# Four later modulation vectors: one row in four column groups, spread through memory

## The chip, the cores and the metric

The kernel runs on one core of a Trainium2 chip. The core has a matrix engine (TensorE, PE in the profile; its weight loads are listed apart as PEld), a vector engine (VectorE, DVE), an activation engine (ScalarE, ACT), a general engine (GpSimd, POOL) and an engine that here does nothing but issue transfers (SyncE, SP). Each of them takes its instructions in the order in which the program wrote them and waits where a semaphore says so. The metric is the time of one execution on the device, in microseconds (us); lower is better.

## The reference, cut to what matters

```python
mod = (_silu(c) @ w_mod).reshape(c.shape[0], 6, 1, -1)      # c: 1x512, w_mod: 512x3072
sa, ca, ga, sb, cb, gb = (mod[:, 0], mod[:, 1], mod[:, 2], mod[:, 3], mod[:, 4], mod[:, 5])
h = _layernorm(x, axis=-1) * (1 + ca) + sa                  # x: 1x2048x512
x = x + ga * _A_ref(h, A_wqkv, A_wo)                        # softmax attention, 32 heads of 16
h = _layernorm(x, axis=-1) * (1 + cb) + sb
x = x + gb * _B_ref(h, B_w1, B_b1, B_w2)                    # dense 512 -> 1792, mish, dense -> 512
return x
```

The six modulation vectors of 512 numbers each are numbered 0 to 5 in the kernel: `sa`, `ca` are 0 and 1, the gate `ga` is 2, the second shift `sb` is 3, the second scale `cb` is 4, the gate `gb` is 5. All of it is in float32; the large products take each operand as a high and a low part and add three products.

## The kernel before, in words

The kernel has a prologue (norm, transposes, the first K and Q slices), one long loop, and a tail. The loop goes in steps. A step of the main part makes, for one group of four heads, four score products of 512 columns whose results the activation engine turns into exponentials (lines 587 and 590), and beside them four more for a later group, of which the vector engine takes row maxima (lines 538 and 540). Two at a time stand on the two halves of the array's rows, and the results go through a ring of six PSUM banks. The step ends with `pv` (line 605): four float32 products of the exponentials with V, each in its own group of 32 array columns. In the slots beside the score products lies a unit of other work, cut in pieces: here the remaining Q, K and V slices (line 138, or line 131 outside the slots).

What is to be done beside the steps is hung on half-steps: `at(h, f)` runs `f` when the writing of the program comes to half-step `h`. All engines' programs are written in this one order, and there is no scheduler behind it. The transfers are all issued by SP, in the order in which they were written; with each the program also waits until the transfer that SP issued eight places earlier has landed, since eight completion slots are used in turn.

The modulation vectors 0 and 1 are made in the prologue. The other four are made in the loop, one after the other, in the order `(2, 5, 3, 4)`. For each, two pieces of `w_mod` are loaded (`mod_load`, line 699; `wm`), GpSimd multiplies them by `silu(c)` and adds the four row blocks (lines 703 to 705), which leaves a 128x512 tile whose columns are still to be summed over the 128 partitions. Six half-steps after the second piece `mod_unit` is written as a special at the end of a step, just ahead of `pv`. It sums over partitions on the matrix engine, into one bank of the ring:

- for a gate (2 and 5) the weights are a 128x128 tile of ones and the tile streams through, twice 256 columns. Every partition then holds the whole vector, and the activation engine copies the bank into the tile `gate` (line 722);
- for shift and scale (3 and 4) the tile itself is the weights, four blocks of 128x128, and one column of ones streams through each. The 512 sums then lie down the partitions in four columns, and the vector engine copies them into `modc` (lines 724 and 726).

Gate 0 is multiplied into the output weights and gate 1 into the second dense layer's weights (`prep_unit`, line 737), which are prepared in the loop later; columns 2 and 3 of `modc` are used when the second norm is applied (line 922). After the last of the four vectors `start_preps` begins the chain of these preparations.

Of the kernel before, what the change touches and what calls it, by code (L numbers as in the profile page):

```python
# [8 lines left out]
F32 = mybir.dt.float32  # L9
F32R = mybir.dt.float32r  # L10
AF = mybir.ActivationFunctionType
# [7 lines left out]
def adaln_block(ctx: ExitStack, tc: tile.TileContext, x, wqkv, wo, w1, b1, w2, c, w_mod, out):  # L19
    nc = tc.nc  # L20
    P = 128
    S, D = x.shape[1], x.shape[2]
# [3 lines left out]
    DK = D // P  # L26
# [27 lines left out]
    dram = ctx.enter_context(tc.tile_pool(name="dram", bufs=1, space=DRAM))  # L54
# [18 lines left out]
    ones = cst.tile([P, 1], F32, name="ones")  # L73
# [9 lines left out]
    modc = cst.tile([P, 4, DK], F32, name="modc")  # L83
    sil = cst.tile([P, DK], F32, name="sil")
    b1c = cst.tile([P, FT], F32, name="b1c")
    gates = [cst.tile([P, D], F32, name=f"gate{i}") for i in range(2)]

    def dap(t, off, ap):
        return bass.AP(tensor=t.tensor, offset=t.offset + off, ap=ap)
# [36 lines left out]
    def mm(acc, l, r, start, stop):  # L126
        pe_queue.append((acc, l, r, start, stop))
# [27 lines left out]
    def ring(w=1):  # L155
        if w == 2 and ring_at[0] % 2:
            ring_at[0] += 1
        if kept and ring_at[0] % NRING == NRING - 1:
            ring_at[0] += 1
        b = ring_at[0] % NRING  # L160
        ring_at[0] += w
        return ring_t[:, b, :] if w == 1 else ring_t[:, b:b + 2, :]
# [41 lines left out]
    def at(h, f):  # L204

        hooks.setdefault(h, []).append(f)
# [22 lines left out]
    def slice_load(kind, i, pool=None, lp=None):  # L229
        w = P if kind < 2 else 2 * P  # L230
        raw = (pool or qp).tile([P, DK, w], F32, tag="raw" if pool is pw else "wr", name="wr", bufs=2 if lp else 1)
        o = kind * D + i * w
        nc.sync.dma_start(raw, wqkv[:, o:o + w].rearrange("(k p) m -> p k m", p=P))
        slices[kind, i] = raw
# [93 lines left out]
    with ExitStack() as es:  # L328
# [121 lines left out]
        for i in range(2):  # L450
            row = lp.tile([P, D], F32, tag="hf", name="row", bufs=6)
# [159 lines left out]
    st, mst = {}, {}  # L611
# [96 lines left out]

    def mod_unit(v):

        gate = v in (2, 5)
        acc, rows = ring(), [mst.pop(("wm", 2 * v + o))[:, 0] for o in range(2)]
        for o, row in enumerate(rows):
            if gate:
                mm(acc[:, o * 2 * P:(o + 1) * 2 * P], ones.to_broadcast([P, P]), row, True, True)
            else:
                for m in range(2):
                    mm(acc[:, 2 * o + m:2 * o + m + 1], row[:, m * P:(m + 1) * P], ones, True, True)

        def fin(h):  # L720
            if gate:
                nc.scalar.copy(gates[(v - 2) // 3], acc)
            elif v == 4:
                nc.vector.tensor_scalar_add(modc[:, v - 1, :], acc[:, :DK], 1.0)
            else:
                nc.vector.tensor_copy(modc[:, v - 1, :], acc[:, :DK])
        return fin

    def prep_unit(h, third, scr, src, gate):
# [683 lines left out]
        return fin  # L1413

    at(-2 * PRO, lambda: slice_load(*plan[2][1:3]))
    order = (2, 5, 3, 4)

    def first_mods(h, j=0):
        for o in range(2):
# [2 lines left out]
    def queue_mod(j):  # L1422
        def make():
            put = mod_unit(order[j])

            def fin(h):
                put(h)
                if j + 1 < len(order):
                    first_mods(h, j + 1)
                else:  # L1430
                    start_preps(h + 2)
            return fin

        queue_special(lambda: mst.get(("row at", 2 * order[j] + 1), 4 * T) + 6, make)
# [110 lines left out]
```

## Time and profile before

| what | value |
|---|---|
| time, median of 3 runs | 1693.89 us (1693.4 to 1694.09) |
| the profiled execution's own time | 1694.02 us |
| its span, first to last instruction | 1692.1 us |
| granted TensorE clock, mean | 0.999 |
| PE / DVE / ACT / POOL busy | 1671.4 / 1442.0 / 1354.5 / 821.1 us |
| transfers | 238.44 MB, mean 141 GB/s |

In rows of the timeline the first column is the start in us from the span's start, the second the length in us, then engine, line, operation, written tile, read tiles, array tile where the engine is PE (64*128 is half of the array's rows, 128*32 a group of 32 columns), shapes and count; in brackets stands how long the engine was idle before, and what ended it. A float32 product appears as two records of PE, so the four products of `pv` are eight. Rows of consecutive records of the same line are merged.

### The profile page before, as it was taken

To read this page: it belongs to the slowest core of one execution; us is meant where nothing else is said; L and a number is where in the kernel's file an instruction comes from. 1 tells how busy PE (TensorE), PEld (TensorE's weight loads), DVE (VectorE), ACT (ScalarE), POOL (GpSimd) and SP (SyncE) were. 2 spreads that over 40 slices of the span, in tenths; PEclk is the share of its full clock that TensorE was granted. 3 is DMA by queue.
4 is the path that set the end of the run, shared out by engine and by line. 5 is a ranking of instruction groups with operands and counts; after the bars stand their busy time and mean duration, and the time that the engine had idled before them with its cause. 6 is when DMAs were issued, how large, how long until landed. Compare 5 with 4: busy or idle time off the path is not lost.

```text
span 1692.1 us, 33739 instructions
## 1 busy us (share of the span) xinstructions
PE 1671.4 (99%) x12410; PEld 925.8 (55%) x12410; DVE 1442.0 (85%) x2371; ACT 1354.5 (80%) x2610; POOL 821.1 (49%) x843
## 2 busy tenths in 40 slices
PE   7999999999999999999999999999999999999999
PEld 5755665555444555555555455555555455555587
DVE  8888888888889888888889888888889888884377
ACT  6257777777778988888888998888888998888674
POOL 7556224665413564555323564555323565555443
PEclk9999999999999999999999999999999999999999
DMA  7877545777755343434355434424354533533261
GB/s 250 260 239 201 132 136 179 229 224 216 216 172 142 106 101 84 127 80 131 85 145 148 118 74 97 137 73 132 82 146 126 131 93 77 143 107 128 77 230 63
DMA packets 114029, 238.44 MB, mean 141 GB/s; under 512 B 23824, under 2 KB 49424, under 8 KB 107912
## 3 DMA queue, kind: packets, MB, share of 16 engines
q1 hardware_dynamic: 113864, 236.28, 49.5%
q8 instruction: 98, 1.61, 0.4%
q14 instruction: 67, 0.55, 0.1%
HBM read 179.95 MB, written 51.44 MB: 137 GB/s over the span
## 4 chain that ended last, share of the span: by engine, by line
PE 92%; DVE 3%; ACT 3%; DMA 1%; issue 1%; POOL 1%; SPq 0%; ACTq 0%; DVEq 0%; POOLq 0%
PE bk L605 29%; PE ring L587 22%; PE ring L538 20%; PE bk L138 10%; PE bk L131 3%; PE ring L131 2%; PE ring L1214 2%; DVE mx L540 2%; ACT pr L590 1%; PE ring L552 1%; DMA xt<-in_A_x 0%; PE ring L917 0%; PE ring L567 0%; PE ring L138 0%; DMA ka<-kscr 0%
## 5 line engine op out<-in xcount | busy, mean ns | idle before, releaser
L540 DVE TENSOR_REDUCE mx<-ring 128x1 f32<-128x512 f32 x1968 | 1222.9, 683 | 151.3 <-PE ring L538 137.9
L590 ACT ACTIVATE pr<-ring 128x512 f32<-128x512 f32 x2048 | 1078.3, 603 | 209.3 <-PE bk L138 116.4
L538 PE MATMUL ring<-ka,qa 64*128 64x512 f32 x1968 | 818.6, 429 | 1.3 <-ACT pr L590 1.1
L587 PE MATMUL ring<-qa,ka 64*128 64x512 f32 x2048 | 759.4, 402 | 2.2 <-ACT pr L590 2.0
L605 PE MATMUL bk<-pr,vg 128*32 128x512 f32 x4096 | 545.1, 605 | 0.0
L538 PEld LDWEIGHTS ring<-ka,qa 64*128 64x128 f32 x1968 | 350.8, 184 | 326.2 <-DVE mx L540 251.3
L587 PEld LDWEIGHTS ring<-qa,ka 64*128 64x128 f32 x2048 | 374.0, 184 | 193.1 <-DVE mx L540 112.2
L138 PE MATMUL bk<-h,w 64*128 64x512 f32 (+1 forms) x1080 | 278.1, 391 | 0.0
L138 PE MATMUL bk<-w,a_h 64*128 64x512 f32 x632 | 211.0, 413 | 0.0
L138 PEld LDWEIGHTS bk<-h,w 64*128 64x128 f32 x1080 | 178.8, 185 | 8.4 <-ACT pr L590 1.5
L605 PEld LDWEIGHTS bk<-pr,vg 128*32 128x32 f32 x4096 | 80.8, 108 | 136.1 <-issue 126.6
L138 PE MATMUL bk<-w,a_l 64*128 64x512 f32 x316 | 124.3, 393 | 0.0
L138 PEld LDWEIGHTS bk<-w,a_h 64*128 64x128 f32 x632 | 106.9, 185 | 3.9 <-ACT hb L795 0.8
L973 POOL TENSOR_TENSOR y<-yd,y 128x512 f32<-128x512 f32 x44 | 56.9, 1292 | 89.1 <-ACT yd L972 84.2
L807 POOL TENSOR_SCALAR qq<-ee 128x512 f32<-128x512 f32 x25 | 15.5, 619 | 169.3 <-ACT ee L801 169.3
L823 POOL TENSOR_TENSOR qq<-qq,rr 128x512 f32<-128x512 f32 x42 | 54.2, 1289 | 86.0 <-ACT rr L817 86.0
L809 POOL TENSOR_TENSOR hb<-hb,ee 128x512 f32<-128x512 f32 x42 | 54.1, 1289 | 79.6 <-DVE ee L805 77.7
L138 PE MATMUL bk<-w,o_hl 64*128 64x512 f32 x288 | 79.1, 405 | 0.0
L100 POOL TENSOR_TENSOR a_l<-hb,a_h 128x512 fp32r<-128x512 f32 x53 | 73.2, 1381 | 4.4
L138 PEld LDWEIGHTS bk<-w,a_l 64*128 64x128 f32 x316 | 58.4, 185 | 3.2
L97 POOL TENSOR_SCALAR qh<-qf 128x512 fp32r<-128x512 f32 x27 | 16.7, 620 | 88.9 <-ACT qf L261 75.2
L138 PE MATMUL bk<-h_h,wl 64*128 64x512 f32 x168 | 57.2, 420 | 0.2 <-ACT pr L590 0.2
(222 smaller groups left out, 1917.0 us busy)
## 6 DMA issues: line engine op xcount, KB each, us to landing
ka<-kscr SPq DMA_DIRECT2D x124, 384.0 KB
w<-w2scr SPq DMA_DIRECT2D x56, 512.0 KB
w<-w1scr SPq DMA_DIRECT2D x46, 512.0 KB
vg<-vscr SPq DMA_DIRECT2D x32, 552.0 KB
qa<-qscr SPq DMA_DIRECT2D x124, 100.0 KB
kscr<-qh SPq DMA_DIRECT2D x16, 512.0 KB
qscr<-qh SPq DMA_DIRECT2D x32, 256.0 KB
w2scr<-hl SPq DMA_DIRECT2D x14, 512.0 KB
```

The source lines that it names most:

```text
L100: (nc.gpsimd if eng == "p" else nc.vector).tensor_sub(lo, src, hi.bitcast(F32))
L131: nc.tensor.matmul(acc, l, r, start=start, stop=stop)
L138: i = nc.tensor.matmul(acc, l[64 * g:64 * g + 64], r[64 * g:64 * g + 64], start=start and not then, stop=bool(stop and then))
L538: nc.tensor.matmul(pm, qt[64 * s:64 * s + 64, qs * P:(qs + 1) * P], kt[64 * s:64 * s + 64, kb * TB:(kb + 1) * TB], start=True, stop=True)
L540: nc.vector.tensor_reduce(out=mxs[n][:, s, 4 * j + qs, kb:kb + 1], in_=pm, op=ALU.max, axis=AX.X)
L587: nc.tensor.matmul(p_, kt[64 * s:64 * s + 64, kc * P:(kc + 1) * P], qt[64 * s:64 * s + 64, :], start=True, stop=True)
L590: e = nc.scalar.activation(pr, p_, AF.Exp, scale=SCALE)
L605: nc.tensor.matmul(accs[n][32 * h:32 * h + 32, :], vgs[n][:, o:o + 32], pts.pop((t, h)), start=(kc == 0), stop=(kc == 15))
L809: (nc.vector if tail else nc.gpsimd).tensor_mul(hb, hb, ee)
L823: nc.gpsimd.tensor_mul(qq, qq, rr)
L973: nc.gpsimd.tensor_add(y[i], yd, y[i])
L1214: nc.tensor.matmul(po[i // 2][:, i % 2, :], l[:, s], w[:, r, :], start=(f == 0 and j == 0), stop=(f == FT - 1 and j == 2))
```

## The change

All four vectors now take the same path. The weights are a 128x32 tile of ones, and the four blocks of 128 columns of the summed tile stream through the four groups of 32 array columns, one block each. The bank then holds, in partitions 0, 32, 64 and 96, the four quarters of the vector (repeated in the 31 partitions behind each). The activation engine copies 128x128 of it into the first 128 columns of a gate tile (for vector 4 with one added). Two half-steps later a transfer takes the four partitions to a new scratch in memory, `mscr`, and ten half-steps after that a second transfer brings them back: for a gate as a row repeated on all 128 partitions, for shift and scale number by number into a column of `modc`. The order of the four vectors becomes `(3, 4, 2, 5)`, so that the gate tiles are free to hold the rows of shift and scale first.

```diff
     gates = [cst.tile([P, D], F32, name=f"gate{i}") for i in range(2)]
+    mscr = dram.tile([4, DK, P], F32, name="mscr")
...
     def mod_unit(v):
-        gate = v in (2, 5)
-        acc, rows = ring(), [mst.pop(("wm", 2 * v + o))[:, 0] for o in range(2)]
-        for o, row in enumerate(rows):
-            if gate:
-                mm(acc[:, o * 2 * P:(o + 1) * 2 * P], ones.to_broadcast([P, P]), row, True, True)
+        acc, ws = ring(), [mst.pop(("wm", 2 * v + o)) for o in range(2)]
+        rows, modt = [w[:, 0] for w in ws], gates[v // 4][:, :P]
+        for c in range(DK):
+            mm(acc[32 * c:32 * c + 32, :P], ones.to_broadcast([P, 32]), rows[c // 2][:, c % 2 * P:(c % 2 + 1) * P], True, True)
+
+        def fin(h):
+            if v == 4:
+                nc.scalar.activation(modt, acc[:, :P], AF.Identity, bias=ones)
             else:
-                for m in range(2):
-                    mm(acc[:, 2 * o + m:2 * o + m + 1], row[:, m * P:(m + 1) * P], ones, True, True)
-
-        def fin(h):
-            if gate:
-                nc.scalar.copy(gates[(v - 2) // 3], acc)
-            elif v == 4:
-                nc.vector.tensor_scalar_add(modc[:, v - 1, :], acc[:, :DK], 1.0)
-            else:
-                nc.vector.tensor_copy(modc[:, v - 1, :], acc[:, :DK])
+                nc.scalar.copy(modt, acc[:, :P])
+            dst = mscr[v - 2]
+
+            def spread():
+                if v in (2, 5):
+                    nc.sync.dma_start(gates[(v - 2) // 3], dap(dst, 0, [[0, P], [1, D]]))
+                else:
+                    nc.sync.dma_start(modc[:, v - 1, :], dst.rearrange("k p -> p k"))
+
+            at(h + 2, lambda: nc.sync.dma_start(dst, modt[::32, :]))
+            at(h + 12, spread)
         return fin
...
-    order = (2, 5, 3, 4)
+    order = (3, 4, 2, 5)
```

On the matrix engine the four blocks stay where they were, ahead of a `pv`. The third of them before the change, with the tile `wm` as weights and the ones streaming (rows name the written tile, then weights and streamed tile, then partitions by columns of the result; `ka`, `qa` are the K and Q tiles of the score products, `bk<-pr,vg` is `pv`):

```order
L587 MATMUL ring<-qa_108,ka_629 128x512
L587 MATMUL ring<-qa_109,ka_630 128x512
L538 MATMUL ring<-ka_104,qa_106 128x512
L131 MATMUL ring<-ones,wm 128x1 x4
L605 MATMUL bk<-pr,vg 32x512 x4
L587 MATMUL ring<-qa_109,ka_630 128x512
```

The same place after the change, where all line numbers are one higher:

```order
L588 MATMUL ring<-qa_109,ka_630 128x512
L588 MATMUL ring<-qa_110,ka_631 128x512
L539 MATMUL ring<-ka_105,qa_107 128x512
L132 MATMUL ring<-wm,ones 32x128 x4
L606 MATMUL bk<-pr,vg 32x512 x4
L588 MATMUL ring<-qa_110,ka_631 128x512
```

Nothing moved there; the four products are now of the same form as those of `pv`, 32 partitions each, and only 128 columns long.

On SP eight transfers come in. Before, between the second and the third vector's load, the last of four small transfers into a Q tile (`qa<-mt`), a load of weights (`wr`), and the loads of a pair of Q and K tiles for a later group of heads:

```order
L576 DMA qa_109<-mt 2x4x128
L233 DMA wr<-in_A_wqkv 128x4x128
L312 DMA qa_106<-qscr 50x512 x2
L321 DMA ka_104<-kscr 48x2048 x2
L699 DMA wm<-in_w_mod 128x4x256 x2
```

After:

```order
L577 DMA qa_110<-mt 2x4x128
L728 DMA modc<-mscr 128x4x1
L234 DMA wr<-in_A_wqkv 128x4x128
L313 DMA qa_107<-qscr 50x512 x2
L322 DMA ka_105<-kscr 48x2048 x2
```

The way back of the first vector, from memory into `modc`, now stands ahead of the loads of the pair (whose tiles are numbered one higher); its way out stands eight transfers earlier, ahead of a load of V. The other three vectors' transfers come in likewise in the next 70 us, and all others keep their order.

## Prediction

> **What bounds the kernel now.** I read the page first: the span, the busy shares, the chain that ended last.
>
> ```profile
> span 1692.1 us, 33739 instructions
> PE 1671.4 (99%) x12410; PEld 925.8 (55%) x12410; DVE 1442.0 (85%) x2371; ACT 1354.5 (80%) x2610; POOL 821.1 (49%) x843
> PE 92%; DVE 3%; ACT 3%; DMA 1%; issue 1%; POOL 1%; SPq 0%; ACTq 0%; DVEq 0%; POOLq 0%
> ```
>
> PE is busy in 99% of the span and holds 92% of the chain. A busy PE can still be waiting inside a stage, so I went to the stage that the change touches. The four vectors are summed between 124 and 199 us, and there the matrix engine's timeline tells the cost:
>
> ```profile
> 121.44 0.40 PE L538 MATMUL ring<-ka,qa 64*128 64x512 f32 x1
> 121.77 1.07 PE L605 MATMUL bk<-pr,vg 128*32 128x512 f32 x8
> ...
> 124.73 1.10 PE L131 MATMUL ring<-wm,ones 128*128 128x256 f32 x4
> 125.77 1.06 PE L605 MATMUL bk<-pr,vg 128*32 128x512 f32 x8
> ...
> 128.60 1.06 PE L605 MATMUL bk<-pr,vg 128*32 128x512 f32 x8
> ...
> 140.08 1.07 PE L605 MATMUL bk<-pr,vg 128*32 128x512 f32 x8
> 141.08 0.28 PE L567 MATMUL ring<-ident,mm 128*32 128x128 f32 x1
> 141.29 0.50 PE L538 MATMUL ring<-ka,qa 64*128 64x512 f32 x1
> ...
> 146.04 1.06 PE L605 MATMUL bk<-pr,vg 128*32 128x512 f32 x8
> ...
> 148.54 0.47 PE L538 MATMUL ring<-ka,qa 64*128 64x512 f32 x1
> 149.01 1.10 PE L131 MATMUL ring<-wm,ones 128*128 128x256 f32 x4
> 150.04 1.06 PE L605 MATMUL bk<-pr,vg 128*32 128x512 f32 x8
> ...
> 152.88 1.07 PE L605 MATMUL bk<-pr,vg 128*32 128x512 f32 x8
> ```
>
> The start of line 605 is the clock tick of a step. Four plain steps run from 128.60 to 140.08, so a plain step is 2.87 us. The steps that hold a gate's sum run from 121.77 to 125.77 and from 146.04 to 150.04: 4.00 each, 1.13 more than plain. The same two ticks for shift and scale:
>
> ```profile
> 170.13 1.06 PE L605 MATMUL bk<-pr,vg 128*32 128x512 f32 x8
> ...
> 173.09 1.02 PE L131 MATMUL ring<-ones,wm 128*128 128x1 f32 x8
> 174.04 1.06 PE L605 MATMUL bk<-pr,vg 128*32 128x512 f32 x8
> ...
> 194.36 1.07 PE L605 MATMUL bk<-pr,vg 128*32 128x512 f32 x8
> ...
> 197.32 1.02 PE L131 MATMUL ring<-ones,wm 128*128 128x1 f32 x8
> 198.27 1.07 PE L605 MATMUL bk<-pr,vg 128*32 128x512 f32 x8
> ```
>
> Both take 3.91, 1.04 more than plain. So all of a block's length lies on the path, and nothing else hides it: 1.13 + 1.13 + 1.04 + 1.04 = 4.34 us for the four. The steps just behind run a little faster than plain (125.77 to 128.60 is 2.83, 150.04 to 152.88 is 2.84), because the other engines have caught up; that gives back 0.03 to 0.04 a block, so the blocks cost 4.2 net. This is the most that the change can win on the matrix engine, and 0.25% of the time.
>
> **The matrix engine's part.** Removed are 4 records of 256 columns in each gate block and 8 records of one column, each with a full 128x128 weight load, in the others. Added are, in every block, 8 records of 128 columns in four column groups of 32. Their price is not in the trace, but the same form is, four times longer, in line 605. Its eight records seen in stretches (busy time, with the number of records under way in brackets, for PE and for the weight loads):
>
> ```profile
> 125.74:125.90 0.16, 0.13 (x4) 0.14 (x8) 1.00 0.00 0
> 125.90:126.22 0.32, 0.32 (x4) 0.02 (x4) 1.00 0.00 0
> 126.22:126.42 0.20, 0.20 (x8) 0.00 (x0) 1.00 0.00 0
> ```
>
> The four groups run at once: four records are under way from 125.77, the next four join at about 126.24, 0.47 later, and the eight weight loads are over in 0.16. The granted clock is 1.00. Line 605 as a whole holds the path for 1.00 (140.08 to 141.08). With 128 columns in place of 512 a wave's pitch is 0.47 / 4 = 0.12, two waves 0.24; what 605 has beyond two pitches (1.00 - 0.94 = 0.06) I keep whole. That gives 0.30 a block. Bounds: from below 0.21, what one lone record of 128 columns behind 32-wide weights holds (line 567, 141.08 to 141.29). From above the groups do not overlap and the eight records go at the pace of the eight one-column records of the old shift block (173.09 to 174.04, 0.12 each), which is 0.95 and wins almost nothing. I take 0.30, since line 605 is the nearest row: same array tile, same type, the same stream into four groups of one bank.
>
> The block also stands next to `pv`, which now has its form. The old block began 0.47 behind the last score product (148.54 to 149.01), `pv` alone begins 0.33 behind it (121.44 to 121.77). By block lengths only (from line 131's start to line 605's: 1.04, 1.04, 0.95, 0.95, together 3.98) the gain would be 3.98 - 1.2 = 2.8; by the steps, which also count those 0.14, it is 4.2 - 1.2 = 3.0. The Trainium skill (TensorEngine Tiling (Array Packing), Key Properties) says that a change of the tiling mode drains the array, while another tile of the same mode does not; the old order changes mode twice from score products to `pv`, the new one once. By that rule the 0.14 go too, and the trace's 0.47 against 0.33 agrees. I take 3.0.
>
> **The activation engine's part.** Two copies of 128x512 go, four of 128x128 come, and two small vector-engine copies go.
>
> ```profile
> 149.32 0.59 ACT L261 COPY qf<-bk 128x512 f32<-128x512 f32 x1
> 149.79 0.63 ACT L590 ACTIVATE pr<-ring 128x512 f32<-128x512 f32 x1
> 150.28 0.62 ACT L722 COPY gate<-ring 128x512 f32<-128x512 f32 x1
> 151.56 2.06 ACT L590 ACTIVATE pr<-ring 128x512 f32<-128x512 f32 x4 [0.67 <-PE ring L538]
> ```
>
> ```profile
> L290 ACT COPY vq<-bk x28: 367/370/395, 53.7 to 244.9; 128x256 f32<-128x256 f32 x28
> ```
>
> 512 columns cost 0.62 and 256 cost 0.37, so 128 cost about 0.25: 4 x 0.25 = 1.0 against 1.24. Cost at nothing: behind the gate copy ACT idles 0.67 until the next step's scores come. With the block 0.8 shorter these come at 150.8 instead of 151.56, while the copy ends at 150.28 + 0.25 = 150.53; 0.2 to spare. For the one copy with a bias I allow 0.46 (line 922, below, has scale and bias on the same shape); it ends at 150.74, still in time. If that cover is gone ACT is next to be late, by 0.2 at most a block, 0.8 in all. A gain beyond the block's length has no place here, since ACT waits for PE.
>
> **The eight transfers.** SP issues them, and behind each stands what SP has queued. Who would notice are the K and Q tiles that the score products wait for.
>
> ```profile
> 149.49 0.77 SPq L321 DMA_DIRECT2D ka<-kscr  x2
> ...
> 155.50 2.62 SPq L271 DMA_DIRECT2D qscr<-qh  x2
> ```
>
> ```profile
> L331 SPq DMA_DIRECT2D cc<-in_c x1: 449/449/449, 0.7 to 0.7; - x1
> L360 ACT ACTIVATE sil_e<-cc x1: 205/205/205, 2.9 to 2.9; 128x4 f32<-128x4 f32 x1
> ```
>
> ```profile
> 149.00:164.00 15.00, 15.00 (x142) 9.48 (x143) 11.91 (x20) 12.20 (x25) 8.62 (x8) 1.00 0.97 214
> ```
>
> ```profile
> 182.00:196.00 14.00, 14.00 (x138) 8.70 (x138) 12.48 (x24) 10.47 (x22) 3.50 (x3) 1.00 0.09 25
> ```
>
> The columns before the last two are busy engines and the clock; then come the DMA share and GB/s. `cc` is of the same form as the way back into `modc` (512 pieces of four bytes): issued at 0.7, in use at 2.9, so at most 2.2 us to land. It stands before the busy stretch of 149 to 164. The write of four half-kilobyte rows has 10 half-steps, 5 x 2.87 = 14 us, to land before it is read back. A gate's spread is 256 KB, at the 214 GB/s of the stretch 1.2 us; the first falls into 182 to 196, where transfers fill 9%. An issue costs SP about 0.45 (`cc`'s row). The new readers have time:
>
> ```profile
> L737 POOL TENSOR_TENSOR hl<-hl,gate x18: 1267/1278/1290, 293.7 to 451.1; 128x512 f32<-128x512 f32 x18
> L922 ACT ACTIVATE hf<-ring,modc x48: 448/462/487, 518.1 to 1297.3; 128x128 f32<-128x128 f32 x48
> ```
>
> Gates are first read at 293.7 and `modc` at 518.1, the last spread is issued six steps behind the last block, near 198 + 6 x 2.87 = 215. Cost: 0, between 0 and the rival below. The new order of the vectors costs nothing for the same reason. As eight slots are used in turn and eight transfers are added, all later transfers keep their slots.
>
> **Sum.** 4 x 0.30 - 4.2 = -3.0 us. The profiled execution took 1694.02 (1.9 around its span of 1692.1), the median is 1693.89; I subtract from the median: 1690.9.
>
> **Rivals.**
>
> *The block nearly vanishes.* The weight loads hide behind the stream and only two pitches remain, 0.22 to 0.24. Then the four steps save 4.34 - 0.9 = 3.4 to 3.5 and the time is 1690.4. For it: eight loads take 0.16 in all in line 605 and lie beside the stream. Against it: one record of line 567 alone holds 0.21. It decides from 0.24 a block downwards. A fifth of a per cent, 3.4 us, is about what a measurement of this kernel can tell from no change, so this is the case on the far side of that line.
>
> *The groups do not overlap, or ACT's copies hold the ring.* Then blocks are 0.95 or steps stay near 3.9, the gain is 0.1 to 1 and the time 1693.3. Against it: line 605's x4 rows. It is also the case that the change does not do what it says.
>
> *Slower: a pair of K and Q tiles comes late.* The K tile issued from 149.49 has landed by 155.50 + 2.62 = 158.1 (line 271 waits for its completion slots), and the first product on it is due at 162.5: the tick at 146.04, a long step, four plain ones and a `pv` (146.04 + 4.00 + 4 x 2.87 + 1.00). That leaves 4.4; with PE 1.5 earlier, 2.9. If small pieces clogged the queue in a stretch already 97% full, the steps would stand. To end slower by 0.2% the pair must be late by 2.9 + 3.0 + 3.4 = 9.3 us; at that point the time is 1697.3. For it: the full stretch. Against it: `cc`'s 2.2. The Trainium skill (DMA: Bandwidth & Descriptors, Specifications) says that pieces under 512 bytes are read, modified and written; that would make the pieces dearer, and no run here shows how much.
>
> **How the numbers follow.** The forecast, 2.2 to 3.4 saved, 0.55; nearly vanishing, 0.25; no overlap or ACT in the way, 0.12; slower, 0.08. Faster by over 0.2% is the second case, 0.25; within 0.2% are the first and third, 0.67; slower 0.08. The range reaches down to 1689.9 (the whole 4.2 gone would be 1689.7) and up to 1693.2, where the case without overlap begins; what lies outside is most of that and the slower one.
>
> **What would show it.** Right: blocks of eight records `wm,ones` of form 128*32 and 128x128, about 0.3 from their start to line 606's; ticks of 3.15 to 3.2 in these four steps; ACT's copies near 0.25 with idle time behind them; no new wait of line 539 or 588 on `ka` or `qa`; all steps after 205 us as before, 3 us earlier. Wrong: blocks near 0.95; a gap on PE around 160 or 210 us released by a transfer; or steps elsewhere that lengthen by as much.

## The result: 2.5 us less, and what the profile shows after

The median went from 1693.6 us (22 runs) to 1691.1 us (22 runs, 1690.0 to 1695.6): a ratio of 0.9987, 95% interval 0.9981 to 0.9993. That is 0.13% faster (0.07 to 0.19%): a gain, and inside the 0.2% that was called no change. The profiled execution took 1691.02 us. The page of the kernel after:

```profile
span 1689.2 us, 33772 instructions
PE 1667.3 (99%) x12418; PEld 921.5 (55%) x12418; DVE 1441.5 (85%) x2369; ACT 1355.1 (80%) x2612; POOL 821.1 (49%) x843
PE 91%; DVE 3%; ACT 3%; DMA 2%; POOL 1%; issue 1%; SPq 0%; ACTq 0%; DVEq 0%; POOLq 0%
```

PE's share of the chain of waits fell from 92 to 91%, that of transfers rose from 1 to 2%: a first hint that something was given back. The timeline of PE around the second and the third block (all line numbers are one higher, so `pv` is line 606 and the block line 132):

```profile
143.80 1.06 PE L606 MATMUL bk<-pr,vg 128*32 128x512 f32 x8
...
146.30 0.47 PE L539 MATMUL ring<-ka,qa 64*128 64x512 f32 x1
146.76 0.43 PE L132 MATMUL ring<-wm,ones 128*32 128x128 f32 x8
146.98 1.07 PE L606 MATMUL bk<-pr,vg 128*32 128x512 f32 x8
...
149.83 1.07 PE L606 MATMUL bk<-pr,vg 128*32 128x512 f32 x8
...
167.07 1.06 PE L606 MATMUL bk<-pr,vg 128*32 128x512 f32 x8
...
169.60 0.43 PE L539 MATMUL ring<-ka,qa 64*128 64x512 f32 x1
170.03 0.42 PE L132 MATMUL ring<-wm,ones 128*32 128x128 f32 x8
170.25 1.07 PE L606 MATMUL bk<-pr,vg 128*32 128x512 f32 x8
```

From tick to tick these steps take 3.18 (143.80 to 146.98, 167.07 to 170.25), where they took 4.00 and 3.91. From the block's start to `pv`'s there are 0.22 in both: two waves of 0.11, where a wave is four records, one in each column group, that run at once. The lead, from the last score product to the block, is 0.46 (146.30 to 146.76), where it was 0.47.

The activation engine beside the same two blocks:

```profile
147.55 0.63 ACT L591 ACTIVATE pr<-ring 128x512 f32<-128x512 f32 x1
148.04 0.39 ACT L719 ACTIVATE gate<-ring,ones 128x128 f32<-128x128 f32 x1
148.52 2.07 ACT L591 ACTIVATE pr<-ring 128x512 f32<-128x512 f32 x4
...
171.13 0.28 ACT L721 COPY gate<-ring 128x128 f32<-128x128 f32 x1
171.78 2.06 ACT L591 ACTIVATE pr<-ring 128x512 f32<-128x512 f32 x4 [0.37 <-PE ring L539]
```

A plain copy takes 0.28 and ACT then idles 0.37 until the next scores. The copy with a bias takes 0.39; it ends 0.09 before the next exponential starts, so it is just in time. On SP, with four of the eight transfers:

```profile
160.17 0.52 SPq L730 DMA_DIRECT2D mscr<-gate  x1
167.84 0.50 SPq L728 DMA_DIRECT2D modc<-mscr  x1
...
189.38 0.39 SPq L726 DMA_DIRECT2D gate<-mscr  x1
200.02 0.55 SPq L730 DMA_DIRECT2D mscr<-gate  x1
```

Their issues cost SP 0.39 to 0.55 each, and no engine waited for one of the eight. One wait of PE for a transfer is in the trace, though, far behind the blocks, and the first trace of before has none there:

```profile
380.46 0.47 PE L588 MATMUL ring<-qa,ka 64*128 64x512 f32 x1 [1.24 <-DMA qa<-mt]
```

A product of scores waits 1.24 us for the small transfers (`qa<-mt`) that put four maxima into a Q tile. What this wait has to do with the change is the second question of the experiments; the first is what the block and the transfers cost each by itself.

### The profile page after: what moved, and what is told of

The parts are those of the page before. It is cut to its first block, busy times and chain, and to the rows that moved or that the text cites. A ratio compares the mean times of both kernels' runs of the same rounds, so it can differ in the third digit from the quotient of the medians.

```text
span 1689.2 us, 33772 instructions
## 1 busy us (share of the span) xinstructions
PE 1667.3 (99%) x12418; PEld 921.5 (55%) x12418; DVE 1441.5 (85%) x2369; ACT 1355.1 (80%) x2612; POOL 821.1 (49%) x843
## 4 chain that ended last, share of the span: by engine, by line
PE 91%; DVE 3%; ACT 3%; DMA 2%; POOL 1%; issue 1%; SPq 0%; ACTq 0%; DVEq 0%; POOLq 0%
PE bk L606 29%; PE ring L588 22%; PE ring L539 20%; PE bk L139 11%; PE bk L132 3%; PE ring L1219 2%; PE ring L132 2%; DVE mx L541 2%; ACT pr L591 1%; PE ring L553 0%; DMA qa<-mt 0%; DMA xt<-in_A_x 0%; PE ring L922 0%; DMA kscr<-qh 0%; PE ring L568 0%
```

## The experiments

In all of them the ticks (the starts of `pv`) are compared one by one with those of the first trace of before. That splits a kernel's distance from it into parts: the first tick, which lies before the first product, copy or transfer that the change alters; the gain between the first tick and the 35th (near 210 us), which holds the four blocks; what is lost between the ticks near 377 and 432 us, where the waits of PE for transfers lie; and all else up to the last tick, where a gain is positive and a loss negative. The whole table first, in us:

| kernel | first tick at | gain over the four blocks | lost near 380 to 430 | all else | median, and ratio to before |
|---|---|---|---|---|---|
| before, first trace | 110.36 | 0 | 0 | 0 | |
| before_again | 111.74 | 0.04 | 0.02 | 0.00 | 1695.37 (1 run) |
| before_third | 109.08 | 0.04 | 1.18 | -0.10 | 1693.97 (1 run) |
| before_fourth | 109.53 | -0.02 | 2.39 | -0.40 | 1695.98 (1 run) |
| after | 108.95 | 3.13 | 1.19 | -0.16 | 1691.11, 0.9987 (0.9981 to 0.9993) |
| again | 110.61 | 3.17 | 1.36 | -0.14 | 1691.71, 0.9983 (0.9973 to 0.9992) |
| again_third | 110.45 | 3.14 | 0.34 | -0.30 | 1691.79 (1 run) |
| no_transfers | 109.69 | 3.16 | 1.09 | 0.16 | 1690.61, 0.9973 (0.9963 to 0.9983) |
| transfers_only | 109.45 | 0.02 | 0.60 | -0.28 | 1694.55, 0.9994 (0.9985 to 1.0004) |
| behind_pv | 109.94 | 3.41 | 0.63 | -0.23 | 1691.52, 0.9982 (0.9972 to 0.9992) |
| double_block | 109.47 | 2.30 | 0.53 | -0.29 | 1691.84 (1 run) |
| two_groups | 113.34 | 1.70 | 1.78 | -0.12 | 1697.41 (1 run) |
| long_block | 111.28 | -0.35 | 0.88 | -0.24 | 1696.61 (1 run) |

The ratios are to the kernel before run beside each: 1693.6 for the first result, 1694.84 (28 runs) for again, no_transfers, transfers_only and behind_pv. Of the others one run of before stood beside: 1695.59 with double_block, two_groups, before_again and before_third, and 1694.05 with long_block, before_fourth and again_third, which ran on another chip. The first tick alone varies by 2.7 us between traces of the same kernel (109.08 to 111.74 for before). The gain over the blocks repeats to 0.04 us. So single times say little here, and the column of the blocks says much. The after of the first result has 1.4 us from its prologue that the change didn't give.

**The change once more (again).** The kernel after, unaltered, timed beside the three that follow.

> The changed kernel unaltered, once more. In its first trace the four blocks save 3.1 us against the trace of before, the prologue ended 1.4 us earlier, and 1.3 us were given back at 379 us, where a score product waited 1.2 for a transfer into a Q tile (`qa<-mt`). Theory of the blocks: the four long steps are again 3.18 to 3.19 long. If the prologue's 1.4 and the wait at 379 are chance of one execution, at least one of them is different here; if they belong to the change, both are there again within 0.2.

Measured: steps of 3.17 and 3.18, 3.17 us over the four blocks, ratio 0.9983. The gain of a block is a fixed thing; its sum over four is 3.1 to 3.2. Neither the earlier prologue (the first tick is at 110.61) nor the wait at 379 us came again. In its place PE waits twice further on, once for a K tile:

```profile
416.21 0.47 PE L539 MATMUL ring<-ka,qa 64*128 64x512 f32 x1 [0.42 <-DMA ka<-kscr]
428.34 0.46 PE L588 MATMUL ring<-qa,ka 64*128 64x512 f32 x1 [0.65 <-DMA qa<-mt]
```

**The transfers left out (no_transfers).** The eight transfers go, and what they would fill, beyond the 128 columns that the copies write, is set to ones, so the gates, the second shift and the second scale are left out of the computation.

```diff
-            at(h + 2, lambda: nc.sync.dma_start(dst, modt[::32, :]))
-            at(h + 12, spread)
...
+    def fill():
+        for g in gates:
+            nc.gpsimd.memset(g[:, P:], 1.0)
+        nc.gpsimd.memset(modc[:, 2:4, :], 1.0)
+
+    at(10, fill)
```

> The changed kernel without its eight transfers: the rows stay in the gate tiles, so gates and the second shift and scale hold other numbers, filled in by three short GpSimd writes; the output is not the reference's. If the transfers are hidden: the four steps stay at 3.18, nothing else moves, and the time is that of the changed kernel within 0.5 us. If they cost (rival): it is 1 us or more faster than the changed kernel, and the wait on `qa<-mt` near 379 us is gone.

Measured: the same 3.16 over the blocks, and the wait on `qa<-mt` is there without any of the eight transfers:

```profile
381.32 0.47 PE L588 MATMUL ring<-qa,ka 64*128 64x512 f32 x1 [1.15 <-DMA qa<-mt]
```

So neither the gain nor that wait comes from the transfers. The median is 1.1 us below that of again, but the two intervals overlap (0.9963 to 0.9983 against 0.9973 to 0.9992), and the trace shows 0.3 to 0.5 of it in "all else" (0.16 against -0.14 and -0.30). Two steps near 668 and 850 us, 0.57 together, are longer in again and not here (the last section returns to them). What the eight transfers cost is therefore somewhere from 0 to 1 us.

**The transfers alone (transfers_only).** The old blocks, copies and order of vectors, with eight transfers of the same sizes through a scratch of the same form; the two small ones end in a spare tile. The edit, against the kernel before:

```diff
+            j = order.index(v)
+            dst = mscr[j]
...
+                    nc.sync.dma_start(spare_c[:, j, :], dst.rearrange("k p -> p k"))
...
+                at(h + 2, lambda: nc.sync.dma_start(dst, gates[j][::32, :P]))
+            at(h + 12, spread)
```

> The kernel before, with eight transfers added on the same half-steps and of the same sizes (out of a gate tile to memory; back into spare columns, for the gates the same values into the same tile). If the transfers are hidden: steps of 4.00, 4.00, 3.91, 3.91 as before, and the time of before within 0.5 us. If transfers cost: 1 us or more slower than before, with a wait on a transfer in the matrix engine's rows.

Measured: ratio 0.9994 (0.9985 to 1.0004), steps of 4.00 and 3.92 as before. Added to the old kernel, the transfers can't be told from nothing. With the run above this leaves the 3.1 us to the blocks, with their copies and their order; long_block below singles out a block's length.

**The block twice (double_block).** The four products are written two times over.

```diff
-        for c in range(DK):
+        for c in (0, 1, 2, 3, 0, 1, 2, 3):
```

> The changed kernel with the four products of each block made twice, so 16 records where there were 8. It prices a block without its lead. If the four column groups run at once: two more waves of 0.11 to 0.12 each, steps of 3.40 to 3.42 in place of 3.18. If the groups go one behind the other and the 0.22 seen is only a pace of starts (0.027 a record): also 0.22 more, but the records then would not be four at a time in the stretches. If the starts are short and the work comes later, in `pv`: more than 0.3 more.

Its timeline of PE at the second block:

```profile
147.01 0.48 PE L539 MATMUL ring<-ka,qa 64*128 64x512 f32 x1
147.49 0.64 PE L132 MATMUL ring<-wm,ones 128*32 128x128 f32 x16
147.92 1.07 PE L606 MATMUL bk<-pr,vg 128*32 128x512 f32 x8
```

Sixteen records take 0.43 where eight took 0.22, and the steps 3.39 to 3.40 where they took 3.18. The sixteen start in fours, at 147.49, 147.60, 147.71 and 147.82 by the single records of the trace, so the groups do run at once. A wave of four groups is 0.11, and `pv`'s first wave in the same trace is 0.43 (its second starts at 148.35): four times the columns, four times the time, so there is hardly a fixed cost within the block.

**Two column groups (two_groups).** The same streams into two groups of 64 columns, 256 columns each; the copy and the way out are fitted to it.

```diff
-            mm(acc[32 * c:32 * c + 32, :P], ones.to_broadcast([P, 32]), rows[c // 2][:, c % 2 * P:(c % 2 + 1) * P], True, True)
+            mm(acc[64 * c:64 * c + 64, :2 * P], ones.to_broadcast([P, 64]), rows[c], True, True)
```

> The changed kernel with two column groups of 64 in place of four of 32: two products of 256 columns a block, which run at once (four records, two waves of 256 columns), rows of 256 numbers in partitions 0 and 64, copies of 128x256. The block then differs in its tile from `pv` behind it. By the streams alone it lasts 2 x 0.22 = 0.43 to 0.45 from its start to `pv`, and steps are 3.40. If a change of the array's tiling costs the 0.13 that I put on it, it lasts 0.56 or more and steps are 3.53.

```profile
151.05 0.48 PE L539 MATMUL ring<-ka,qa 64*128 64x512 f32 x1
151.52 0.65 PE L132 MATMUL ring<-wm,ones 128*64 128x256 f32 x4
152.10 1.06 PE L606 MATMUL bk<-pr,vg 128*32 128x512 f32 x8
```

This streams as many column waves as the doubled block (two of 256 columns against four of 128), but holds 0.58 (151.52 to 152.10) instead of 0.43. By the single records its two waves start at 151.52 and 151.76, 0.24 apart, and `pv` starts 0.35 behind the second. So 0.11 of the 0.15 stands where the tile changes from 128*64 to `pv`'s 128*32; the rest may be a slower wave. The old gate's block shows the like: its records start at 149.01, 149.30, 149.51 and 149.73, the last ones 0.22 apart, and `pv` 0.31 behind the last. The lead ahead of the block is 0.47 again. The Trainium skill (TensorEngine Tiling (Array Packing), Key Properties) says that a change of the tiling mode drains the array and another tile of the same mode doesn't: a drain of about 0.1 would fit the rows here, and between block and `pv` of one mode nothing shows (the new block's second wave starts at 146.87, `pv` 0.11 later). The time of two_groups, 1697.41, is one run that began its loop 3 us late; by its steps (3.54) it would stand 1.4 us behind the change.

**The block behind `pv` (behind_pv).** The special is written after the step's `pv` instead of ahead of it.

```diff
         if not mid:
             pv(t - 2)
+        do_specials(2 * t + 1, True)
...
+    def do_specials(h, late=False):
+        if specials and specials[0][2] == late and h >= specials[0][0]():
```

> The changed kernel with the four blocks moved one place, from ahead of `pv` to behind it. In the changed kernel a block takes 0.22 from its start to `pv`, but starts 0.46 behind the last score product where `pv` alone starts 0.33 behind: the 0.13 did not go with the tiling mode. If the 0.13 are a matter of the switch from score products to a product of full rows with semaphore waits of its own, they stay wherever the block stands: steps stay at 3.15 to 3.2. If they come from the place (the waits for the ring's bank and for GpSimd stand on the path there and are hidden behind the 1.0 of `pv` here): steps fall to about 3.05, 0.5 us in all for the four, and the time is that of the changed kernel less 0.5.

```profile
147.20 0.46 PE L539 MATMUL ring<-ka,qa 64*128 64x512 f32 x1
147.59 1.06 PE L606 MATMUL bk<-pr,vg 128*32 128x512 f32 x8
148.47 0.40 PE L132 MATMUL ring<-wm,ones 128*32 128x128 f32 x8
148.80 0.49 PE L588 MATMUL ring<-qa,ka 64*128 64x512 f32 x1
```

`pv` now follows the scores, and its lead in such a step is 0.39 (147.20 to 147.59). From `pv`'s start to the next score product there are 1.21, against 1.00 without a block, so the block holds 0.21 here too. Over the four blocks 3.41 are won instead of 3.15, 0.06 to 0.07 a block, which is what the lead is shorter (0.39 for 0.46). That is half of what the second case of the expectation gave (0.5 in all), so neither of its two cases holds as it stands. In the time the two places aren't told apart (0.9982 against 0.9983, run side by side).

**Is the wait near 380 us a consequence? (before_again, before_third, before_fourth, again_third, long_block).** Every trace with a short block loses time between 377 and 432 us, most of them at this wait, again and behind_pv only further on (behind_pv 0.70 on `qa<-mt` at 427 us); the first trace of before loses none. Either PE comes 3 us earlier and runs into transfers that don't move, or the wait belongs to the execution, whatever the kernel. First two more traces of before:

> The kernel before, once more, for a second trace of it. All four traces with the short blocks lose 0.5 to 1.3 us between 375 and 435 us against the first trace of before, and so does the kernel before with added transfers (0.5). If the loss belongs to an earlier matrix engine (transfers at 70% and more there, which do not come earlier by as much), this trace shows no loss there against the first one. If it is the chance of one execution, this trace loses 0.5 to 1.3 too.

> As the run ahead of it, a third trace: losses in both would make the first trace of before the exception, in neither would lay them to the change; steps around the four sums are 4.00, 4.00, 3.91 and 3.91 in both.

The first had none, the second 1.16. Then three more, one of them a kernel made for the question: the changed kernel with all its transfers, but with each block five times as long, so that PE comes as late as before.

```diff
-        for c in range(DK):
+        for c in (0, 1, 2, 3) * 5:
```

> The changed kernel, its eight transfers and all; only the block writes its four products five times, so that it is twenty products long. By the pitch that the doubled block showed (0.21 us for four products more) the four steps become 3.18 + 4 x 0.21 = 4.02, the length before the change; the matrix engine is then where it was, with everything else as after. Theory A, an earlier matrix engine runs into the transfer to qa near 380 us: the wait of line 588 on qa<-mt there (1.2 us in the changed kernel) is gone, as in the kernel before. Theory B, the wait belongs to the execution (it stood in one of three traces of the kernel before): it can appear here too, with 0.5 us or more. Theory C, the eight transfers bring it: it appears here with about 1 us. Time by A 1694, by B 1694 to 1695, by C 1695.

> The kernel before, one more trace. Theory A (the wait on qa<-mt near 380 us needs an earlier matrix engine): no wait there, or under 0.3 us; 1694. Theory B (it belongs to the execution): a wait of 0.5 us or more is as likely as not.

> The changed kernel, one more trace. The four steps 3.18 each; Theory A: the wait on qa<-mt near 380 us is there, 0.7 to 1.2 us. Theory B: it may be absent, and the gain of 3.1 us over the four blocks is then kept to the end.

PE of long_block at the block:

```profile
147.00 1.07 PE L606 MATMUL bk<-pr,vg 128*32 128x512 f32 x8
...
149.50 0.47 PE L539 MATMUL ring<-ka,qa 64*128 64x512 f32 x1
149.96 1.30 PE L132 MATMUL ring<-wm,ones 128*32 128x128 f32 x40
151.05 1.07 PE L606 MATMUL bk<-pr,vg 128*32 128x512 f32 x8
```

Ten waves take 1.09, and the step 4.05 (147.00 to 151.05; 4.02 was expected). The gain over the blocks is gone: -0.35. All else in this kernel is as in the changed one, so the gain was the blocks' length. And the wait near 380 us in long_block, then in before_third, then in before_fourth:

```profile
386.02 0.46 PE L588 MATMUL ring<-qa,ka 64*128 64x512 f32 x1 [0.96 <-DMA qa<-mt]
```

```profile
383.82 0.47 PE L587 MATMUL ring<-qa,ka 64*128 64x512 f32 x1 [1.16 <-DMA qa<-mt]
```

```profile
385.62 0.47 PE L587 MATMUL ring<-qa,ka 64*128 64x512 f32 x1 [2.31 <-DMA qa<-mt]
```

In again_third it is 0.41, less than theory A gave. The longest of all thirteen traces stands in the kernel before. The six traces with PE where it was before lose 0.85 on average there (0, 0.02, 1.18, 2.39, 0.60, 0.88), the seven with an earlier PE 0.99 (1.19, 1.36, 0.34, 1.09, 0.63, 0.53, 1.78). So theory A of the last three expectations, that the wait needs an earlier PE, falls, and so does C, that the eight transfers bring it: it belongs to the execution (B). What lets it vary so is not known. The two averages differ by 0.14; as single values go from 0 to 2.39, an effect of PE's place of up to about 1 us (an estimate from this scatter) could still hide in them. The time of long_block, 1696.61, is above what any of the three theories gave, and the table says from where: against the first trace of before it is 0.92 late at its first tick, 0.35 by its blocks, 0.88 at the wait, 0.24 in other steps and 0.2 behind the last tick.

## Why the prediction was right, and what in it was not

1690.9 us were forecast and 1691.1 measured, within the range and within the 0.2% either way. That the two agree so closely is in part luck: the medians differ by 2.5 us (1.2 to 3.2 by the interval) where 3.0 were forecast, and the kernel before came out at 1693.6 in 22 runs where three had given 1693.89. Point by point:

- **All of a block's length lies on the path.** Right. Steps fell from 4.00 and 3.91 to 3.18, and a block made longer on purpose lengthens its step by just as much (0.21 for two waves more in double_block; 4.05 in long_block).
- **The four groups run at once, with a pitch of 0.12.** Right, 0.11. The bound from above (0.95, the groups in a row) is out.
- **A block holds 0.30.** Too long by 0.08. The 0.06 that I kept whole, for what line 605 has beyond two pitches, isn't there: the next `pv` starts right behind the second wave. In behind_pv something like it stands ahead of the score products: `pv` holds 0.88 when the block follows (147.59 to 148.47), and the block 0.33 when scores follow (148.47 to 148.80). The lower bound of 0.21 agrees with the price by chance, since line 567 is one wave with score products behind it and the block is two waves. The block's second wave in behind_pv also holds 0.22 ahead of scores (148.58 to 148.80).
- **The lead's 0.14 go too.** This step failed. The block still begins 0.46 behind the scores, with tiles of 128*32 as with 128*128. I had read 0.47 against 0.33 as the price of the second change of tiling mode. Half of that was never there: plain steps (those without line 567's product) come in two kinds in turn, one of about 2.84 with a lead of 0.32 to 0.36, one of about 2.90 with a lead of 0.36 to 0.41. All four blocks stand in steps of the second kind, and the 0.33 is from the first. Two neighbours, of before:

```profile
131.10 0.47 PE L538 MATMUL ring<-ka,qa 64*128 64x512 f32 x1
131.50 1.07 PE L605 MATMUL bk<-pr,vg 128*32 128x512 f32 x8
...
134.00 0.41 PE L538 MATMUL ring<-ka,qa 64*128 64x512 f32 x1
134.34 1.07 PE L605 MATMUL bk<-pr,vg 128*32 128x512 f32 x8
```

Their leads are 0.40 and 0.34, their steps 2.90 (from 128.60) and 2.84. The other half, 0.06 to 0.07, comes with a block of any tile (128*128, 128*64, 128*32) that stands ahead of `pv`, and goes when it stands behind: the lead in behind_pv, 0.39, is that of a plain step of this kind. A price at a change of tile exists too, 0.11 to 0.15 in two_groups, but it lies between the block and `pv`; in the old kernel it was part of the 1.04 and 0.95 that I took for the block's own length. What the 0.06 to 0.07 are stays open.
- **The sum, -3.0.** It came out at 3.13 to 3.17 in three traces, because two errors nearly cancel. Against a plain step of the same kind, 2.90, an old block cost 1.10 or 1.01, 4.2 for the four, and a new one costs 0.28 (3.18 - 2.90), 1.1 for the four: 0.22 for the block and 0.06 for the lead. The prediction put 0.30 and nothing. Its 4.2 is right, but not for the reason given: the step behind a block is short because it is of the short kind, before and after (146.98 to 149.83, 2.85), and not because other engines have caught up. The sum by the lengths of the blocks, 3.98 - 4 x 0.22 = 3.1, is the right one, as the lead is the same before and after. The prediction had that way (2.8 with 0.30) and took the other.
- **The block nearly vanishes, 1690.4.** Its condition came true (0.22, below its point of 0.24), its time did not: 3.4 to 3.5 was counted against the mean step of 2.87, and as if the block left the lead as it is in a plain step. Against 2.90, and with the lead's 0.06 kept, 0.22 gives 3.1.
- **ACT's copies, about 0.25.** 0.28 and, with the bias, 0.39 where 0.46 was allowed. Hidden, as forecast; behind the copy with bias with next to no margin.
- **The transfers, 0.** Not quite shown. No engine waited for one of them, and with the old blocks they can't be told from nothing; but with the new blocks two steps are longer by 0.57 together in every trace, and without the transfers they are not. The rival of the late pair did not occur: nothing waits near 160 or 210 us. The sign "no new wait on `ka` or `qa`" does not hold to the letter. The waits on `qa<-mt` are in traces of before too, while the one on a K tile (0.42 in again, 416 us) is in that trace alone.
- **All steps later as before, 3 us earlier.** True up to 370 us. After that 0.3 to 1.4 us are lost in waits for transfers, but the kernel before loses 0 to 2.4 there. It blurs single comparisons and isn't shown to be a cost of the change. The two longer steps near 668 and 850 us are one. I took the first trace of before, which has none of it, for typical.

## What to carry to other kernels

On a path with no slack in the matrix engine, cost a small block from the start of its first product to the start of the next instruction, and cost the lead ahead of it apart: a difference between two leads needn't belong to what stands behind it, and where plain steps come in two kinds, compare with one of the same kind. A reduction over partitions whose weights are ones can be cut into column groups and then takes a quarter of the stream, if the way back to the wanted layout has time to go through memory. Before a wait that turns up in the new trace is called a consequence, look for it in three or four traces of the old kernel.

## What the runs showed of the hardware that was not expected

The eight weight loads of the block cost nothing that can be seen: forty records of 128 columns in four groups take 1.09 us, ten waves of 0.109, with a load for each (long_block). Between a block in tiles of 64 columns and `pv` in tiles of 32 stand 0.11 to 0.15 us more than between two of one tile (two_groups).

Two steps of the changed kernel are longer by 0.27 and 0.30 us than before, near 668 and 850 us, in all seven traces that have both the new block and the transfers, and in none of the others (transfers_only has one such step next to the second place); another step, near 607 us, is 0.2 shorter in every kernel but before. At 668 us it is the activation engine that is late. Of before, then of after:

```profile
667.38 1.57 ACT L590 ACTIVATE pr<-ring 128x512 f32<-128x512 f32 x3 [0.83 <-PE ring L587]
668.84 0.69 ACT L795 ACTIVATE hb<-bk,b1c 128x512 f32<-128x512 f32 x1
```

```profile
663.65 1.09 ACT L591 ACTIVATE pr<-ring 128x512 f32<-128x512 f32 x2 [0.84 <-PE ring L588]
...
664.90 0.60 ACT L591 ACTIVATE pr<-ring 128x512 f32<-128x512 f32 x1 [0.16 <-PE ring L539]
```

Three exponentials run without a pause before; after, a pause of 0.16 stands ahead of the third, in the same place of the program each time. The matrix engine named as its releaser was not later than before, so what ended the pause isn't known, and why it comes with code that was changed 450 us earlier was not tried. Two reasons are out by the runs at hand: an earlier PE, since long_block has both steps longer with PE as late as before, and the transfers alone, since transfers_only has neither at its place.
